# Zero-padded fixed buffers for the probabilities, one add per join, and another point for placing transposed keys, in a sliding-window attention and MLP kernel

## The chip, the cores and the metric

The kernel runs on one core of a Trainium2 chip. The metric is the device time of one execution in microseconds. Six executions of the kernel before gave a median of 327.75 us, from 327.45 to 328.67. A core has five engines, each with a queue of its own that it works through in order: TensorE (PE; its weight loads are listed apart as PEld), VectorE (DVE), ScalarE (ACT), GpSimd (POOL) and SyncE (SP, which here only issues DMAs).

## What is computed

Attention over a window of 32 positions to either side, for 8 batches, 8 heads, 576 tokens and 64 features, and then a two-layer MLP over the 4608 tokens:

```python
scores = scale * np.matmul(q, k.transpose(0, 1, 3, 2))
mask = np.abs(pos[:, None] - pos[None, :]) <= window          # window = 32
scores = np.where(mask, scores, -1000000000.0)
attn = np.exp(scores - np.max(scores, axis=-1, keepdims=True))
attn = attn / (np.sum(attn, axis=-1, keepdims=True) + 1e-09)
x = np.matmul(attn, v)                                        # heads side by side: 4608 x 512
h = x @ w_in                                                  # 512 x 2048
out = np.maximum(0.01 * h, h) @ w_out                         # 2048 x 512
```

## The kernel before

**Chunks.** Attention is cut into 64 chunks. A chunk is one batch, one half of its tokens (288) and one pair of heads: chunk i is batch i // 8, half (i // 4) % 2, pair i % 4. The keys of a pair are held in blocks of 64, two heads in one 128 x 128 weight with zeros off the diagonal (`kbd`, and likewise `vbd` for the values), so that one matmul serves both heads. Nine blocks make a sequence. A block of 64 keys meets up to 128 queries, so neighbouring blocks overlap: in a half, the even blocks together cover all 288 queries, and the odd blocks cover 256 of them. A chunk's scores are these two runs side by side, 544 columns (`NCOL`), made by five matmuls (line 242) in the order of the table `WIN` (line 130): even blocks first and odd ones behind, in both halves.

**A chunk's way.** `score` (line 237): five matmuls into PSUM, then ACT takes the exponential (line 248), then POOL multiplies with a band mask of zeros and ones (line 252), which gives the probabilities `pr`, 128 x 544 in bf16. `join` (line 255), from chunk 12 on: DVE adds the odd run to the even one, so that one matmul gives the sums; 256 of the 288 columns are an add of two parts of `pr` (line 263), and the 32 columns that no odd block covers are a copy (line 265). `weighted` (line 268): PE multiplies the joined sums with a matrix of ones (`s`, line 274; for chunks under 12 it does so for the two runs one after the other, lines 276 and 279), and the probabilities with the values (`x`, line 286). DVE takes the reciprocal of `s` (line 292) and multiplies `x` with it into `xT` (line 294). `s` and `x` have one PSUM buffer each, so PE can't write the next `s` before DVE has taken the reciprocal of the last.

**Keys and queries.** They are loaded by SP, cast to bf16 (line 168: on POOL, at the start also on DVE), and transposed: for batches 0 to 2 by PE (line 201), from batch 3 (`BY_DMA`) by DMA (line 187). ACT then copies the transposed queries and keys into token order (lines 209 and 215), and `place_keys` (line 221) has DVE copy each key tile into the two diagonal parts of `kbd` (line 227, two copies). DVE's copy stands in DVE's queue behind what was queued before it, and what comes behind it waits until ACT's copy is there.

**The MLP.** It works on groups of 288 tokens (half a batch): 16 tiles of the hidden layer per group, each four matmuls (line 305) and a leaky ReLU on ACT (line 309), and output tiles of 128 tokens, each 16 matmuls of 512 columns (line 322), evacuated by ACT (line 327) and stored by SP. Its matmuls take most of PE's time, and the attention of later chunks is laid between them.

**Order.** The program's order is each engine's order. A plan (line 494) lists hidden tiles and quarters of output tiles with the time that PE should need for each; before each, `spend` (line 515) takes the attention steps that have come due. `step` (line 361), for chunk i, queues: the join of chunk i+1; the placing of keys that still wait; transposes that are due; the score of chunk i+2 (in batches from 3 on with its keys' transposes and their placing ahead of it); `weighted(i)`; placing again; then casts, DMA transposes and loads for later batches. Beside the steps, in output tiles at every odd turn, `spend` has ACT copy one more tile of queries or keys that a DMA has transposed (line 532), and right behind it `place_keys` is called (line 533). Engines wait for each other by semaphores that are derived from what each instruction reads and writes.

**Buffers.** `pr` and `both` come from a pool of four buffers each (line 52).

Of the kernel before, what the change touches and what calls it, by code (L numbers as in the profile page):

```python
# [10 lines left out]
BF16 = mybir.dt.bfloat16  # L11
AF = mybir.ActivationFunctionType
# [4 lines left out]
def kernel(  # L17
# [12 lines left out]
    nc = tc.nc  # L30

    B, H, S, D = q.shape
    W = 32
    scale = 1.0 / float(D) ** 0.5
# [5 lines left out]
    HALF = S // 2  # L40
    DMC = DMODEL // 128
    FFC = DFF // 128
    NCOL = 544
# [3 lines left out]
    const = ctx.enter_context(tc.tile_pool(name="const", bufs=1))  # L47
    fload = ctx.enter_context(tc.tile_pool(name="fload", bufs=1))
    cast = ctx.enter_context(tc.tile_pool(name="cast", bufs=1))
    attn = ctx.enter_context(tc.tile_pool(name="attn", bufs=2))  # L50
    kt = ctx.enter_context(tc.tile_pool(name="kt", bufs=4))
    prob = ctx.enter_context(tc.tile_pool(name="prob", bufs=4))
    tdma = ctx.enter_context(tc.tile_pool(name="tdma", bufs=1))
    outp = ctx.enter_context(tc.tile_pool(name="outp", bufs=4))
    PS = bass.MemoryType.PSUM
# [48 lines left out]
    ones_bd = const.tile([128, 128], BF16)  # L104
# [13 lines left out]
    def clear(t, p):  # L118
# [8 lines left out]

    WIN = [  # L130
        [(0, 0, 96), (2, 96, 128), (4, 224, 64), (1, 32, 128), (3, 160, 128)],
        [(4, 288, 64), (6, 352, 128), (8, 480, 96), (5, 288, 128), (7, 416, 128)],
    ]
    ODD = [32, 0]

    win = const.tile([128, 3, 128], BF16)
    nc.gpsimd.memset(win, 1.0)
    for lo in (0, 64):
        w = win[lo:lo + 64]
        nc.gpsimd.affine_select(  # L140
            out=w, in_=w, compare_op=ALU.is_ge, fill=0.0,
# [3 lines left out]
            out=w, in_=w, compare_op=ALU.is_ge, fill=0.0,  # L145
            base=2 * W, channel_multiplier=1, pattern=[[0, 3], [-1, 128]],
        )
    win_f = win.rearrange("p n c -> p (n c)")
    mask = [const.tile([128, NCOL], BF16, name=f"mask{i}") for i in range(2)]

    def make_masks():
        for hf in range(2):
            lo = W * (hf + 1)
            nc.gpsimd.tensor_copy(out=mask[hf][:, 0:HALF], in_=win_f[:, lo:lo + HALF])
            nc.gpsimd.tensor_copy(out=mask[hf][:, HALF:NCOL], in_=win_f[:, 0:NCOL - HALF])


    RING = 4 * HALF
# [7 lines left out]
    def cast_qk(b, p, q_eng=None):  # L166
        for eng, src, dst in ((q_eng or nc.gpsimd, qf, qb), (nc.gpsimd, kf, kb)):
            eng.tensor_copy(  # L168
                out=dst[:, p], in_=src[b, p].rearrange("p a (c d) -> p c a d", d=D),
            )  # L170
# [10 lines left out]
    BY_DMA = 3  # L181
    qkT, asked = {}, {}

    def transpose_dma(b, p):
        for which, src in (("q", qb), ("k", kb)):
            t = tdma.tile([128, RUN, 96], BF16, name=f"{which}T{p}")
            nc.sync.dma_start_transpose(out=t, in_=src[:, p].rearrange("p c a d -> p (c a d)"))
            qkT[b, p, which] = t
        asked[b, p] = state["done"]
# [29 lines left out]
    unplaced = []  # L219

    def place_keys():

        while unplaced:
            b, p, kT = unplaced.pop(0)
            for a in range(2):
                r = slice(64 * a, 64 * a + 64)
                nc.vector.tensor_copy(  # L227
                    out=kbd[b % 2][r, p, :, r],
                    in_=kT[r].rearrange("p (n j) -> p n j", j=64),
                )  # L230

    probs = {}

    def where(i):
        return i // 8, (i // 4) % 2, i % 4

    def score(i):
        b, hf, p = where(i)
        ps = scps.tile([128, 1024], FP32, name="ps")
        c0 = 512 - HALF  # L240
        for blk, q0, n in WIN[hf]:
            nc.tensor.matmul(  # L242
                ps[:, c0:c0 + n], kbd[b % 2][:, p, blk],
                qT[b][:, p, q0:q0 + n], start=True, stop=True,
            )
            c0 += n
        e = attn.tile([128, NCOL], BF16, name="e")
        nc.scalar.activation(  # L248
            out=e, in_=ps[:, 512 - HALF:512 - HALF + NCOL], func=AF.Exp, scale=scale,
        )  # L250
        pr = prob.tile([128, NCOL], BF16, name="pr")
        nc.gpsimd.tensor_mul(pr, e, mask[hf])  # L252
        probs[i] = pr, None

    def join(i):


        hf = where(i)[1]
        pr = probs[i][0]
        both = prob.tile([128, HALF], BF16, name="both")  # L260
        o0 = ODD[hf]
        o1 = o0 + NCOL - HALF
        nc.vector.tensor_add(both[:, o0:o1], pr[:, o0:o1], pr[:, HALF:NCOL])  # L263
        rest = slice(0, o0) if o0 else slice(o1, HALF)
        nc.vector.tensor_copy(out=both[:, rest], in_=pr[:, rest])  # L265
        probs[i] = pr, both

    def weighted(i):
        b, hf, p = where(i)
        pr, both = probs.pop(i)  # L270
        x = xps.tile([128, HALF], FP32, name="x")
        s = xps.tile([128, HALF], FP32, name="s")
        if both is not None:
            nc.tensor.matmul(s, ones_bd, both, start=True, stop=True)  # L274
        else:
            nc.tensor.matmul(
                s, ones_bd, pr[:, 0:HALF], start=True, stop=False, skip_group_check=True,
            )
            nc.tensor.matmul(
                s[:, ODD[hf]:ODD[hf] + NCOL - HALF], ones_bd, pr[:, HALF:NCOL],  # L280
                start=False, stop=True, skip_group_check=True,
            )
        c0 = 0
        for n_, (blk, q0, n) in enumerate(WIN[hf]):
            a = q0 - HALF * hf
            nc.tensor.matmul(  # L286
                x[:, a:a + n], vbd[b % 2][:, p, blk, :], pr[:, c0:c0 + n],
                start=(n_ == 0), stop=(n_ == len(WIN[hf]) - 1), skip_group_check=True,
            )
            c0 += n  # L290
        r = attn.tile([128, HALF], FP32, name="r")
        nc.vector.reciprocal(r, s)  # L292
        t0 = (b * S + hf * HALF) % RING
        nc.vector.tensor_mul(xT[:, p, t0:t0 + HALF], x, r)  # L294
# [58 lines left out]
    def step_transposes(upto):  # L353
        while state["tp"] < min(upto, 8 * B):
            b = state["tp"] // 8
            if b not in t_parts:
                t_parts[b] = transposes(b)
            next(t_parts[b])
            state["tp"] += 1

    def step():


        i = state["done"]
        b, r = i // 8, i % 8
        if JOINED - 1 <= i < NC - 1:
            join(i + 1)
        place_keys()
        if b > 0:
            upto = 8 * (b + 1) + (PLAN[b > 1][0][r] if b + 1 < BY_DMA else 0)  # L370
            step_transposes(max(upto - 1, 8 * (b + 1)))
        if i < 7:
            score(i + 1)
        elif 8 <= i < NC - 2:
            nb, _, np_ = where(i + 2)
            if nb >= BY_DMA:
                step_transposes(8 * nb + 2 * np_ + 2)
                place_keys()
            score(i + 2)
        weighted(i)  # L380
        place_keys()
        if b > 0:
            step_transposes(upto)
        if 0 < b < B - 1:
            for p in PLAN[b > 1][1][r] if b + 1 <= BY_DMA else ():
                cast_qk(b + 1, p)
                if b + 1 == BY_DMA:
                    transpose_dma(b + 1, p)
                if b + 2 < B:
                    load_qk(b + 2, p)  # L390

            n, p = (b + 1, 3) if r == 0 else (b + 2, r - 4)
            if p in range(4 if r == 0 else 3) and BY_DMA < n < B:
                step_transposes(8 * (n - 1) + 2 * p + 2)
                place_keys()
                cast_qk(n, p)
                transpose_dma(n, p)
                if n + 1 < B:
                    load_qk(n + 1, p)
            for p in PLAN[b > 1][2][r]:  # L400
                cast_v(b + 1, p)
                if b + 2 < B:
                    load_v(b + 2, p)
        state["done"] += 1
# [97 lines left out]
    at, t = {}, 0.0  # L502
# [10 lines left out]
    turn = 0  # L513

    def spend(us):
        nonlocal clock, turn
        while due and due[0] <= clock:
            due.pop(0)
            i = state["done"]
            if i < 11:  # L520
                cast_v(1, i - 7)

            if i < 12:
                load_qk(2, i - 8)
            step()
            if 10 <= i < 14:
                load_v(2, i - 10)

        b, p = state["tp"] // 8, state["tp"] % 8 // 2
        turn += 1  # L530
        if kind == "o" and turn % 2 and b >= BY_DMA and (b, p, "k") in qkT and state["done"] > asked[b, p] + 2:
            step_transposes(state["tp"] + 1)
            place_keys()
        clock += us

    for us, kind, g, f in plan:
        if kind == "h":
            spend(us)
            h_tile(g, f)
        elif f == 0:  # L540
            o_tile(g, lambda: spend(O_US))
# [28 lines left out]
```

## Time and profile before

The profiled execution took 327.71 us; its span, from the first instruction to the last, was 326.0 us.

| what | value |
| --- | --- |
| median of 6 runs | 327.75 us |
| profiled execution, and its span | 327.71 us, 326.0 us |
| reciprocals (line 292, DVE) | 64 x 1955 ns |
| mask multiplies (line 252, POOL) | 64 x 1216 ns |
| placing of keys (line 227, DVE) | 64 x 446 ns, and 24.9 us of waiting for ACT's key copies |
| reciprocals waiting for PE's `s` (line 274) | 35.5 us, 34 times |
| hidden layer on PE (line 305) | 1024 matmuls, 133.1 us |
| output layer on PE (line 322) | 592 matmuls, 130.1 us |
| granted TensorE clock | full speed throughout |

How to read the views that follow. The page's first part gives the busy time of each engine and its share of the span. In the part on groups, a line has the source line, the engine, the operation, the output and inputs by the program's names, their form, the count, then busy time in all and the mean of one in ns, and after the second bar the time that the engine was idle just before them. The table by stages has, for each stretch of the span, its length and then for PE, PEld, DVE, ACT and POOL the busy time with the number of instructions, and after these the granted clock, the DMA share and GB/s. The list of waits has the waiting line, what it waited for, the total in us, the number of times and the longest. A timeline has start, length, engine, line, operation and count, and in brackets the idle time before it with what ended it. Matmul ends are modelled, so spacings on PE are better read from start to start.

### The profile page before, as it was taken

The page shows a single profiled execution, that of the slowest core. Times are in us where ns is not written, and L with a number is a line of the kernel's source. Part 1 is how long each engine was busy: PE and PEld are TensorE (multiplying, and loading weights), DVE is VectorE, ACT ScalarE, POOL GpSimd, SP SyncE. Part 2 cuts the span into 40 slices and gives each one's busy share as a digit, 9 for nine tenths or more (in the row PEclk, how much of TensorE's full clock was granted, in tenths as well). Part 3 has the DMA queues.
Part 4 walks back from the last instruction along what each step waited for, and adds up shares of the span by engine and source line. Part 5 has one row for each costly group of instructions (what it writes and reads, how often), then busy time and mean ns, then how long its engine had stood idle before and what let it go on. Part 6 is the DMA issues. An engine that isn't in the chain of part 4 may idle for free.

```text
span 326.0 us, 6609 instructions
## 1 busy us (share of the span) xinstructions
PE 306.7 (94%) x2485; PEld 205.3 (63%) x2485; DVE 224.6 (69%) x310; ACT 224.6 (69%) x432; POOL 179.9 (55%) x213
## 2 busy tenths in 40 slices
PE   1587999999999998999999999999999999999995
PEld 1345785576675755667675767666675857676653
DVE  5389843888767969698758979687849766565100
ACT  5684794375668797778788888888785847464531
POOL 6698839859755876239642686259623544230000
PEclk9999999999999999999999999999999999999999
DMA  8999979999999999917995299917711000010101
GB/s 179 207 196 212 268 191 214 228 256 218 211 201 155 271 205 209 220 66 141 174 240 155 66 194 206 217 68 126 192 38 65 35 32 35 12 55 0 66 32 65
DMA packets 85173, 48.28 MB, mean 148 GB/s; under 512 B 64021, under 2 KB 80661, under 8 KB 85141
## 3 DMA queue, kind: packets, MB, share of 16 engines
q1 hardware_dynamic: 80852, 43.66, 64.7%
q0 software_dynamic: 4288, 4.20, 7.8%
q8 instruction: 19, 0.31, 0.4%
q14 instruction: 14, 0.11, 0.1%
HBM read 36.70 MB, written 9.44 MB: 142 GB/s over the span
## 4 chain that ended last, share of the span: by engine, by line
PE 83%; DVE 7%; DMA 3%; SPq 2%; ACT 2%; issue 1%; POOL 1%; DVEq 0%; POOLq 0%; ACTq 0%
PE mm L322 36%; PE mm L305 35%; DVE r L292 5%; PE x L286 4%; PE ps L242 4%; DMA kf<-in_k_dram 3%; PE s L274 2%; PE tp L201 1%; SPq L83 1%; SPq L72 1%; DVE xT L294 1%; ACT kT L215 1%; DVE both L265 1%; DVE kbd L227 1%; POOL kb L168 1%
## 5 line engine op out<-in xcount | busy, mean ns | idle before, releaser
L292 DVE RECIPROCAL r<-s 128x288 f32<-128x288 f32 x64 | 125.1, 1955 | 41.5 <-PE s L274 35.5
L252 POOL TENSOR_TENSOR pr<-e,mask 128x544 bf16<-128x544 bf16 x64 | 77.8, 1216 | 100.6 <-ACT e L248 80.8
L305 PE MATMUL mm<-xT,w_in_bf 128*128 128x288 bf16 x1024 | 133.1, 286 | 0.0
L322 PE MATMUL mm<-w_out_bf,gT 128*128 128x512 bf16 (+2 forms) x592 | 130.1, 373 | 0.0
L309 ACT ACTIVATE gT<-mm 128x288 bf16<-128x288 f32 x256 | 104.1, 412 | 25.4 <-PE mm L305 9.6
L305 PEld LDWEIGHTS <-w_in_bf 128*128 128x128 bf16 x1024 | 98.3, 98 | 23.9
L322 PEld LDWEIGHTS <-gT 128*128 128x128 bf16 x592 | 56.4, 98 | 59.8
L327 ACT ACTIVATE o_sb<-mm 128x512 f32<-128x512 f32 (+2 forms) x37 | 21.7, 585 | 55.6 <-PE mm L322 55.6
L248 ACT ACTIVATE e<-ps 128x544 bf16<-128x544 f32 x64 | 39.8, 622 | 11.1 <-PE ps L242 10.5
L227 DVE COPY kbd<-kT 64x576 bf16<-64x576 bf16 x64 | 28.5, 446 | 25.5 <-ACT kT L215 24.9
L178 POOL CAST vbd<-vf 64x576 bf16<-64x576 f32 x58 | 38.5, 664 | 2.1 <-DMA vf<-in_v_dram 0.3
L294 DVE TENSOR_TENSOR xT<-x,r 128x288 bf16<-128x288 f32 x64 | 29.3, 458 | 6.7
L168 POOL CAST kb<-kf 96x768 bf16<-96x768 f32 x32 | 27.6, 863 | 10.3 <-DMA kf<-in_k_dram 10.3
L286 PE MATMUL x<-pr,vbd 128*128 128x128 bf16 (+2 forms) x320 | 26.3, 214 | 1.3 <-DVE xT L294 1.2
L242 PE MATMUL ps<-qT,kbd 128*128 128x128 bf16 (+2 forms) x320 | 26.8, 216 | 0.0
L242 PEld LDWEIGHTS <-kbd 128*128 128x128 bf16 x320 | 20.9, 101 | 8.2
L286 PEld LDWEIGHTS <-vbd 128*128 128x128 bf16 x320 | 20.9, 99 | 6.6 <-DVE xT L294 2.5
L209 ACT ACTIVATE qT<-qT 128x576 bf16<-128x576 bf16 x20 | 23.6, 1181 | 0.0
L215 ACT ACTIVATE kT<-kT 128x576 bf16<-128x576 bf16 x20 | 23.6, 1180 | 0.0
L265 DVE COPY both<-pr 128x32 bf16<-128x32 bf16 x52 | 22.7, 436 | 0.0
L263 DVE TENSOR_TENSOR both<-pr 128x256 bf16<-128x256 bf16 x52 | 21.0, 405 | 0.6
L168 POOL CAST qb<-qf 96x768 bf16<-96x768 f32 x24 | 19.7, 819 | 0.0
(39 smaller groups left out, 110.9 us busy)
## 6 DMA issues: line engine op xcount, KB each, us to landing
qf<-in_q_dram SPq DMA_DIRECT2D x32, 288.0 KB, 4.5
kf<-in_k_dram SPq DMA_DIRECT2D x32, 288.0 KB, 5.5
vf<-in_v_dram SPq DMA_DIRECT2D x64, 144.0 KB, 5.1
out_dram<-o_sb SPq DMA_DIRECT2D x35, 256.0 KB, 2.2
w_in_bf<-in_moe_w_in_dram POOLq DMA_DIRECT2D x8, 256.0 KB, 6.5
w_out_bf<-in_moe_w_out_dram POOLq DMA_DIRECT2D x4, 512.0 KB, 12.7
qT<-qb SPq DMA_TRANSPOSE x20, 4.3
kT<-kb SPq DMA_TRANSPOSE x20, 3.9
```

The lines of the kernel that those rows point to most:

```text
L168: eng.tensor_copy(out=dst[:, p], in_=src[b, p].rearrange("p a (c d) -> p c a d", d=D),)
L178: nc.gpsimd.tensor_copy(out=vbd[b % 2][r, p, :, r], in_=vf[b, p][r])
L227: nc.vector.tensor_copy(out=kbd[b % 2][r, p, :, r], in_=kT[r].rearrange("p (n j) -> p n j", j=64),)
L242: nc.tensor.matmul(ps[:, c0:c0 + n], kbd[b % 2][:, p, blk], qT[b][:, p, q0:q0 + n], start=True, stop=True,)
L248: nc.scalar.activation(out=e, in_=ps[:, 512 - HALF:512 - HALF + NCOL], func=AF.Exp, scale=scale,)
L252: nc.gpsimd.tensor_mul(pr, e, mask[hf])
L286: nc.tensor.matmul(x[:, a:a + n], vbd[b % 2][:, p, blk, :], pr[:, c0:c0 + n], start=(n_ == 0), stop=(n_ == len(WIN[hf]) - 1), skip_group_c ...
L292: nc.vector.reciprocal(r, s)
L294: nc.vector.tensor_mul(xT[:, p, t0:t0 + HALF], x, r)
L305: nc.tensor.matmul(h[:, 0:HALF], w_in_bf[:, c, ts(f, 128)], xT[:, c, ds(t0, HALF)], start=(c == 0), stop=(c == DMC - 1),)
L309: nc.scalar.activation(out=gT[:, f, ds(t0, HALF)], in_=h[:, 0:HALF], func=AF.Prelu, alpha=0.01,)
L322: nc.tensor.matmul(o[:, lo:hi], gT[:, f, ds(128 * j % RING, 128)], w_out_bf[:, f, lo:hi], start=(f == 0), stop=(f == FFC - 1),)
```

## The change

The probabilities move from the pool into one fixed tile of six buffers, each with 32 columns ahead of the 544 and 32 behind, which are set to zero once. `i % 6` picks the buffer. For the first half, the odd blocks now come first (256 columns) and the even ones behind; for the second half the order stays. With that, the 288 columns that begin in the pad (first half) or end in it (second half) are the odd run with zeros where no odd block reaches, and `join` is one add of 288 columns with 288. `both` gets a pool of its own with two buffers. The masks, the exponential's source and the sums of chunks under 12 follow the new order.

Keys: `step` no longer places at its head from batch 2 on, and places ahead of a score only when a key tile of that very pair waits; and in `spend` a tile whose copy was queued at an odd turn is placed at the next even turn, a quarter of an output tile later in the program.

```diff
+    joined = ctx.enter_context(tc.tile_pool(name="joined", bufs=2))
-    prob = ctx.enter_context(tc.tile_pool(name="prob", bufs=4))
...
+    PAD = 32
+    SPLIT = [HALF - PAD, HALF]
     WIN = [
-        [(0, 0, 96), (2, 96, 128), (4, 224, 64), (1, 32, 128), (3, 160, 128)],
+        [(1, 32, 128), (3, 160, 128), (0, 0, 96), (2, 96, 128), (4, 224, 64)],
         [(4, 288, 64), (6, 352, 128), (8, 480, 96), (5, 288, 128), (7, 416, 128)],
     ]
-    ODD = [32, 0]
...
+    NPROB = 6
+    prob = const.tile([128, NPROB, NCOL + 2 * PAD], BF16)
+    nc.vector.memset(prob[:, :, 0:PAD], 0.0)
+    nc.vector.memset(prob[:, :, PAD + NCOL:], 0.0)
...
     def score(i):
...
-        c0 = 512 - HALF
+        lo = c0 = 512 - SPLIT[hf]
...
         nc.scalar.activation(
-            out=e, in_=ps[:, 512 - HALF:512 - HALF + NCOL], func=AF.Exp, scale=scale,
+            out=e, in_=ps[:, lo:lo + NCOL], func=AF.Exp, scale=scale,
         )
-        pr = prob.tile([128, NCOL], BF16, name="pr")
+        pr = prob[:, i % NPROB, PAD:PAD + NCOL]
         nc.gpsimd.tensor_mul(pr, e, mask[hf])
...
         hf = where(i)[1]
-        pr = probs[i][0]
-        both = prob.tile([128, HALF], BF16, name="both")
-        o0 = ODD[hf]
-        o1 = o0 + NCOL - HALF
-        nc.vector.tensor_add(both[:, o0:o1], pr[:, o0:o1], pr[:, HALF:NCOL])
-        rest = slice(0, o0) if o0 else slice(o1, HALF)
-        nc.vector.tensor_copy(out=both[:, rest], in_=pr[:, rest])
-        probs[i] = pr, both
+        lo = PAD * hf
+        t = prob[:, i % NPROB]
+        both = joined.tile([128, HALF], BF16, name="both")
+        nc.vector.tensor_add(both, t[:, lo:lo + HALF], t[:, lo + HALF:lo + 2 * HALF])
+        probs[i] = probs[i][0], both
...
     def step():
...
-        place_keys()
+        if b < BY_DMA - 1:
+            place_keys()
...
             if nb >= BY_DMA:
                 step_transposes(8 * nb + 2 * np_ + 2)
-                place_keys()
+                if any(key[:2] == (nb, np_) for key in unplaced):
+                    place_keys()
             score(i + 2)
...
     def spend(us):
...
         if kind == "o" and turn % 2 and b >= BY_DMA and (b, p, "k") in qkT and state["done"] > asked[b, p] + 2:
             step_transposes(state["tp"] + 1)
+        elif kind == "o" and turn % 2 == 0:
             place_keys()
```

## The prediction

> **What bounds the kernel now.** I read the engine totals first, then TensorE (PE) by stages, then the list of what PE waited for, and last the instructions of the one stage where it waits.
>
> ```profile
> span 326.0 us, 6609 instructions
> PE 306.7 (94%) x2485; PEld 205.3 (63%) x2485; DVE 224.6 (69%) x310; ACT 224.6 (69%) x432; POOL 179.9 (55%) x213
> ```
>
> PE is at 94%; VectorE (DVE), which the change relieves, is at 69%. So time taken off DVE is worth nothing by itself. It counts only where PE stood still because DVE was late. The stage table gives busy time per stretch (start:end, length, then each engine):
>
> ```profile
> 40.00:124.00 84.00, 83.85 (x717) 55.88 (x716) 59.47 (x84) 59.31 (x119) 60.46 (x71) 1.00 1.04 216
> 124.00:131.00 7.00, 5.29 (x52) 3.75 (x49) 6.75 (x11) 4.44 (x11) 3.74 (x5) 1.00 1.18 198
> 131.00:305.00 174.00, 174.00 (x1380) 116.33 (x1378) 129.64 (x182) 126.58 (x242) 84.02 (x93) 1.00 0.54 110
> ```
>
> PE (first pair) is full from 40 to 124 us and again from 131 to the end of attention. Between them it loses 7.00 - 5.29 = 1.71 us while DVE is busy 6.75 of 7.00. That hole is the only place where a quicker join can pay. The waits of PE from 36 us to the end say the same: nothing but DVE, and little of it.
>
> ```profile
> PE s L274 <- DVE r L292: 1.0, 1, 1.0
> PE x L286 <- DVE xT L294: 0.9, 4, 0.3
> ```
>
> **The hole, instruction by instruction.** The timelines of DVE, POOL and PE over it (start us, length us). Step i handles chunk i: DVE joins chunk i+1, then PE scores i+2 and runs s and x of i, then DVE inverts (r) and multiplies (xT) i.
>
> ```profile
> 120.90 0.91 DVE L227 COPY kbd<-kT 64x576 bf16<-64x576 bf16 x2 [1.55 <-ACT kT L215]
> 121.84 0.29 DVE L263 TENSOR_TENSOR both<-pr 128x256 bf16<-128x256 bf16 x1
> 121.99 1.22 POOL L252 TENSOR_TENSOR pr<-e,mask 128x544 bf16<-128x544 bf16 x1 [1.47 <-issue]
> 122.05 1.19 DVE L265 COPY both<-pr 128x32 bf16<-128x32 bf16 x1
> 123.15 1.94 DVE L292 RECIPROCAL r<-s 128x288 f32<-128x288 f32 x1
> 125.15 0.28 PE L274 MATMUL s<-both,ones_bd 128*128 128x288 bf16 x1 [1.00 <-DVE r L292]
> 125.57 0.90 DVE L227 COPY kbd<-kT 64x576 bf16<-64x576 bf16 x2
> 125.71 0.41 PE L286 MATMUL x<-pr,vbd 128*128 128x96 bf16 x5 [0.28 <-DVE xT L294]
> 126.50 0.81 DVE L263 TENSOR_TENSOR both<-pr 128x256 bf16<-128x256 bf16 x1
> 127.23 0.79 DVE L265 COPY both<-pr 128x32 bf16<-128x32 bf16 x1
> 127.94 1.94 DVE L292 RECIPROCAL r<-s 128x288 f32<-128x288 f32 x1
> 130.50 0.41 PE L286 MATMUL x<-pr,vbd 128*128 128x96 bf16 x5 [0.28 <-DVE xT L294]
> ```
>
> This is chunks 23 to 25. DVE waits for ACT's key copy until 120.88, places keys, joins chunk 24 and only at 123.15 begins the reciprocal whose s was issued at 119.93. The 32-column copy took 1.19 us, against a median of 169 ns (view of the tile `both`): POOL's mask multiply, of 1.22 us, had begun at 121.99, between add and copy. Counted by starts, PE reached s24 at 123.98 (score at 123.74 plus 0.24) and issued it at 125.15: 1.17 lost. x24 lost 125.71 - 125.27 = 0.44; s25 129.94 - 129.63 = 0.31; x25 130.50 - 130.06 = 0.44. Together 2.36 us, a little more than the 1.71 that busy time shows.
>
> **Part 1, one add for add and copy.**
>
> ```profile
> L265 DVE COPY both<-pr 128x32 bf16<-128x32 bf16 x52 | 22.7, 436 | 0.0
> L263 DVE TENSOR_TENSOR both<-pr 128x256 bf16<-128x256 bf16 x52 | 21.0, 405 | 0.6
> ```
>
> Removed: 52 copies, 22.7 us of DVE. The add grows from 256 to 288 columns. Unhindered, add start to reciprocal start is 0.28 us now (106.98 to 107.26), of which the add takes 0.21. The 288-column add is not in the trace: from below it costs no more than the present add; from above, the 128x288 multiply of line 294 (one operand f32 in PSUM) takes 458 ns, +0.18. I take +0.02 (0.21 x 32/256), since the nearest row is the same operation, type and memory. So DVE sheds about 52 x 0.42 = 22 us, nearly all beside a full PE, where it is worth 0. In the hole:
>
> - Join 24 starts at 121.84 as now (its keys come from ACT, unchanged), and the reciprocal at 121.84 + 0.23 = 122.07 instead of 123.15. s24 follows a reciprocal's start by 2.00 (123.15 to 125.15): 124.07, while PE is there at 123.98: loss 0.09. x24 follows it by 2.56 (123.15 to 125.71): 124.63.
> - Place of the next keys 2.42 after the reciprocal: 124.49. Join 25, 0.93 later: 125.42. POOL's next mask multiply runs from 125.19 to the next POOL instruction at 126.35, so this add must wait. Now the add of 126.50 waits likewise for the POOL instruction that hands over at 127.11, and DVE's next starts at 127.23, 0.12 later. So the reciprocal starts at 126.35 + 0.12 + 0.02 = 126.49 instead of 127.94.
> - s25 at 128.49; PE, coming from x24 over 28 matmuls, a score and s (0.24 + 3.43 + 0.24), is there at 128.54: no loss. x25 at 126.49 + 2.56 = 129.05 instead of 130.50.
>
> Sum: 1.45 us earlier. It persists: behind it DVE waits 1.80 us for PE before the reciprocal of 135.23, and PE is full to the end.
>
> At this place a rule speaks against counting on the join. The row: the add's longest is 809 ns, its shortest 279. The Trainium skill, page "SBUF — State Buffer", section "Who interferes with whom", says that a DVE instruction with two SBUF inputs contends with a GpSimd instruction that reads SBUF, and the one that comes second is blocked for the other's whole length. The trace agrees (809 is no intrinsic length); by the rule the change halves the occasions but not the price of one, and if each of the two joins met a whole 1.22 us multiply the sum would be a gain of about 0.6 instead of 1.45.
>
> **Part 2, keys placed later.** Writing out, from the two programs, what each engine is given in which order: PE, ACT, POOL and SP get the same order. On DVE, of 52 joins and the placements, four pairs change places. Placements 2,1 and 2,2 (batch, pair) go ahead of joins 16 and 17; their keys leave ACT at 77.88 and 83.30, before DVE is free (79.10 and 84.16), and the reciprocals after them wait for PE anyway (0.66 at 81.72, 1.78 at 87.53): 0. Placements 5,1 and 7,2 go behind a join and a reciprocal, at 172 and 244 us; there DVE stood 2.74 us waiting for ACT, beside a full PE: 0 on the path. Their keys are first read five or six steps later (chunks 41 and 58). If that cover were gone, each would cost at most its own 0.9 us. Elsewhere, a placement queued a quarter of an output tile later, with no DVE instruction between, runs at the same instant. In the hole DVE's order is unchanged. No DMA is issued earlier or later.
>
> **Part 3, buffers.** Two memsets of 192 columns at the start, before the first query cast (4.60). Not in the trace; 64 columns cost 112 ns and 2304 cost 1978, so 0.11 to 0.25 each. The first key transposes wait for POOL until 6.01 and the next for DMA (0.70 at 9.21): 0; uncovered, 0.5. Six buffers instead of four, and two for the joined sums: join i+1 needs s of i-1 done, and DVE has already waited for it in its reciprocal: 0.
>
> **Part 4, order of blocks in the first half.** The same widths, now ending with the 64-wide one instead of 128. Below: nothing to gain. Above: weight loads follow each other by 0.063 us (five in 0.35 at 106.83, the last of 0.098), a 64-wide matmul by about 0.029 (0.2156 us per 512 and 0.1225 per 288 columns give 0.42 ns a column and 2.5 ns): 0.034 x 64 = 2.2 us. I take 0: the group takes 0.24 in both halves (110.62 to 110.86, 115.14 to 115.38), with the 64-wide matmul first in one and third in the other.
>
> **Forecast.** The profiled execution took 327.71 us (span 326.0, 1.7 around it), close to the median of 327.75; less 1.45 gives 326.3, 0.44% faster. About 0.2% (0.66 us) is what a measurement can tell from no change.
>
> **Rivals.**
> - *POOL first at join 24.* The multiply of 121.99 starts 0.15 us after the add; were it first, the reciprocal would start at 123.15 + 0.14, s24 at 125.29, and the second join would wait for the handover at 127.11: reciprocal 127.25, x25 at 129.89. Gain 0.6: 327.1. Against it: both start times hang on the same ACT copy ending at 120.88. Chance 0.12.
> - *Join 25 meets no POOL* (the multiply comes after 125.42): x25 at PE's own pace, 128.65, gain 1.85: 325.9. It needs a shift of only 0.23. Chance 0.13.
> - *Weight loads behind the 64-wide matmul show.* In the 32 first-half chunks, score and x lose up to 0.034 each: 327.71 - 1.45 + 2.2 = 328.5, slower; it decides from 1.45/64 = 0.023 a time, and passes 0.2% at 0.033. Half of it gives about 327.4. Chances 0.09 and 0.06.
> - *The change isn't what it says: one fixed tile is tracked as a whole.* Then x of chunk i would wait for the mask multiply of i+2: exp 0.62 and multiply 1.21 after each score, some 1.9 us x 54 steps, about 430 us. Against it: kbd, xT and gT are single tiles too, and PE reads one part while others write the rest without a wait. Chance 0.05.
> - The forecast has the rest: 0.55.
>
> Faster 0.55 + 0.13 = 0.68; same 0.12 + 0.06 = 0.18; slower 0.14. The range takes in the forecast with its bounds (an add of 458 ns leaves 1.45 - 0.36 = 1.1), both joins' cases, and half the loads: 325.5 to 327.4.
>
> **What would show it.** Right: line 265 gone, its add near 0.30 unhindered, DVE down by some 20 us, PE's idle between 124 and 131 us down from 1.71 to about 0.6 (x24 and x25 still wait for DVE), the end of everything behind it 1.4 to 1.5 earlier, DVE's wait for ACT's keys smaller only at two places. Wrong: a score or x group of a first half taking more than 0.24; the add at chunk 24 lasting over 1 us; a new wait of PE elsewhere.

## The result, and the profile after

The changed kernel takes 325.1 us (median of 21 executions, 324.06 to 326.0) against 327.42 for the kernel before (47 executions): ratio 0.9928, 95% interval 0.9917 to 0.9940, which is 2.4 us less (2.0 to 2.7). The forecast was 326.3 with a range of 325.5 to 327.4; the direction and the place of the gain were right, its size was not.

The totals of the changed kernel's page, and its table by stages (stretch, length, then busy time of PE, PEld, DVE, ACT and POOL with instruction counts, granted clock, DMA share, GB/s):

```profile
span 323.7 us, 6565 instructions
PE 306.2 (95%) x2485; PEld 205.4 (63%) x2485; DVE 208.9 (65%) x260; ACT 224.6 (69%) x432; POOL 180.2 (56%) x213
```

```profile
40.00:124.00 84.00, 83.51 (x713) 55.44 (x711) 55.69 (x72) 59.47 (x119) 60.98 (x71) 1.00 1.01 217
124.00:131.00 7.00, 6.75 (x63) 5.41 (x64) 6.75 (x9) 5.21 (x13) 4.04 (x4) 1.00 1.22 243
131.00:303.00 172.00, 172.00 (x1364) 114.69 (x1363) 117.57 (x144) 125.28 (x239) 83.20 (x92) 1.00 0.50 109
```

PE's busy time is what it was; the hole, 5.29 busy of 7.00 before, is nearly closed: its head now lies just ahead of 124 us, and from 123 to 130 PE is busy for 6.50 of 7.00. PE's waits from 36 us on, where `s` stood with 1.0 us and `x` with 0.9:

```profile
PE x L295 <- DVE xT L303: 0.7, 3, 0.3
```

The join, as a group (busy us, mean ns) and by the view of its tile (shortest, median, longest ns):

```profile
L273 DVE TENSOR_TENSOR both<-prob 128x288 bf16<-128x288 bf16 x52 | 22.8, 439 | 0.6
```

```profile
L273 DVE TENSOR_TENSOR both<-prob x52: 296/309/1146, 63.2 to 292.4; 128x288 bf16<-128x288 bf16 x52
```

43.7 us of add and copy became 22.8; a 288-column add takes 17 ns more than one of 256 had (296 against 279). DVE's total fell by only 15.7, mainly since each copy began before its add had ended (by 0.08 us in the prediction's rows) and the sums of groups count that twice. And the hole (start, length; chunks 23 to 25, as the prediction showed them):

```profile
120.29 0.91 DVE L238 COPY kbd<-kT 64x576 bf16<-64x576 bf16 x2 [1.54 <-ACT kT L226]
121.23 0.31 DVE L273 TENSOR_TENSOR both<-prob 128x288 bf16<-128x288 bf16 x1
121.40 1.22 POOL L263 TENSOR_TENSOR prob<-e,mask 128x544 bf16<-128x544 bf16 x1 [1.45 <-issue]
121.46 1.95 DVE L301 RECIPROCAL r<-s 128x288 f32<-128x288 f32 x1
123.14 0.40 PE L253 MATMUL ps<-qT,kbd 128*128 128x128 bf16 x5
123.46 0.28 PE L282 MATMUL s<-both,ones_bd 128*128 128x288 bf16 x1
124.03 0.41 PE L295 MATMUL x<-prob,vbd 128*128 128x128 bf16 x5 [0.28 <-DVE xT L303]
124.82 1.15 DVE L273 TENSOR_TENSOR both<-prob 128x288 bf16<-128x288 bf16 x1
125.89 1.94 DVE L301 RECIPROCAL r<-s 128x288 f32<-128x288 f32 x1
128.45 0.41 PE L295 MATMUL x<-prob,vbd 128*128 128x128 bf16 x5 [0.22 <-DVE xT L303]
```

Join 24 starts 0.17 us ahead of POOL's multiply and is through; join 25 meets the next multiply and lasts 1.15. Measured from the hole's score (123.74 before, 123.14 after) to x of chunk 25, the hole took 6.76 us and takes 5.31: 1.45 less, the forecast sum. So two profiles that differ by 2.3 us hold 1.45 in the hole; 0.60 had come before its head, and the last 0.24 comes behind PE's last matmul. The experiments ask what the rest is.

### The profile page after: what moved, and what is told of

Its sections match the earlier page's. It is cut to its first block, busy times and chain, and to the rows that moved or that the text cites. A ratio compares the mean times of both kernels' runs of the same rounds, so it can differ in the third digit from the quotient of the medians.

```text
span 323.7 us, 6565 instructions
## 1 busy us (share of the span) xinstructions
PE 306.2 (95%) x2485; PEld 205.4 (63%) x2485; DVE 208.9 (65%) x260; ACT 224.6 (69%) x432; POOL 180.2 (56%) x213
## 4 chain that ended last, share of the span: by engine, by line
PE 79%; DMA 7%; DVE 6%; SPq 2%; ACT 2%; POOL 1%; issue 1%; DVEq 0%; POOLq 0%; ACTq 0%
PE mm L331 36%; PE mm L314 32%; DMA kf<-in_k_dram 7%; DVE r L301 4%; PE x L295 4%; PE ps L253 4%; PE s L282 2%; SPq L72 1%; SPq L83 1%; PE tp L212 1%; DVE xT L303 1%; POOL kb L179 1%; ACT kT L226 1%; DVE kbd L238 1%; DVE both L273 0%
## 5 line engine op out<-in xcount | busy, mean ns | idle before, releaser
L263 POOL TENSOR_TENSOR prob<-e,mask 128x544 bf16<-128x544 bf16 x64 | 77.7, 1214 | 98.7 <-ACT e L259 80.3
L238 DVE COPY kbd<-kT 64x576 bf16<-64x576 bf16 x64 | 28.5, 446 | 20.6 <-ACT kT L226 17.9
L295 PE MATMUL x<-prob,vbd 128*128 128x128 bf16 (+2 forms) x320 | 26.3, 214 | 1.4 <-DVE xT L303 1.3
L253 PEld LDWEIGHTS <-kbd 128*128 128x128 bf16 x320 | 21.8, 101 | 8.0
L295 PEld LDWEIGHTS <-vbd 128*128 128x128 bf16 x320 | 21.8, 99 | 5.1 <-issue 1.9
L273 DVE TENSOR_TENSOR both<-prob 128x288 bf16<-128x288 bf16 x52 | 22.8, 439 | 0.6
L282 PE MATMUL s<-both,ones_bd 128*128 128x288 bf16 x52 | 14.9, 286 | 0.0
```

Source lines behind the costliest of these rows:

```text
L238: nc.vector.tensor_copy(out=kbd[b % 2][r, p, :, r], in_=kT[r].rearrange("p (n j) -> p n j", j=64),)
L253: nc.tensor.matmul(ps[:, c0:c0 + n], kbd[b % 2][:, p, blk], qT[b][:, p, q0:q0 + n], start=True, stop=True,)
L295: nc.tensor.matmul(x[:, a:a + n], vbd[b % 2][:, p, blk, :], pr[:, c0:c0 + n], start=(n_ == 0), stop=(n_ == len(WIN[hf]) - 1), skip_group_c ...
```

## The experiments

Theories: **hole only** (1.45 us is the change, the rest is scatter of the start); **start** (the new buffers, memsets or block order also shorten the first 36 us); **placement** (the later keys carry the rest); and, after the first runs, **amplified** (a microsecond in the hole is worth more in the time). "Stretch" is the hole from its score to x of chunk 25. e12, the kernel before with an unused tile of the new buffers' size and the two memsets, has no result: there is no room for that tile beside the old buffers.

| kernel | stretch, us | median, us | ratio to before, 95% interval |
| --- | --- | --- | --- |
| before again (e1) | 6.76 | 327.36 | 1.0003 (0.9984 to 1.0022) |
| join only (e2) | 5.31 | 324.80 | 0.9939 (0.9917 to 0.9961) |
| placement only (e3) | 6.76 | 327.06 | 0.9999 (0.9978 to 1.0020) |
| all, but add and copy (e4) | 6.76 | 327.02 | 1.0000 (0.9984 to 1.0016) |
| all, but add and copy at 24, 25 (e5) | 6.76 | 327.26 | 0.9991 (0.9970 to 1.0011) |
| one add at 24, 25 only (e6) | 5.32 | 325.28 | 0.9940 (0.9916 to 0.9964) |
| all, a key behind the reciprocal (e7) | 4.40 | 324.02 | 0.9910 (0.9879 to 0.9941) |
| all, again (e8) | 5.31 | 325.30 | 0.9945 (0.9921 to 0.9968) |
| three more reciprocals (e9) | 12.68 | 332.68 | 1.0165 (1.0136 to 1.0194) |
| old join, a key behind (e10) | 5.17 | 325.70 | 0.9949 (0.9929 to 0.9969) |
| e7 again (e11) | 4.39 | 324.70 | 0.9918 (0.9894 to 0.9943) |
| all, tile in another pool (e13) | 5.31 | 325.78 | 0.9949 (0.9928 to 0.9970) |
| block order only (e14) | 6.76 | 327.17 | 0.9993 (0.9977 to 1.0008) |
| all, third time (e15) | 5.31 | 325.35 | 0.9927 (0.9903 to 0.9951) |

**Parts of the change.** e1 is the kernel before.

> The kernel before, unchanged, for a second profile and for how far two sets of runs of one program lie apart. The measured gain of the change (2.3 us) is 0.9 more than the 1.45 us seen in the hole of chunks 23 to 25; in the two profiles 0.6 of it lies before 36 us, where the changed kernel's first loads landed earlier. If that 0.6 is chance (theory: hole only), this second profile shows the first hidden-layer matmul anywhere between 28.0 and 28.8 us, and the ratio is 1.000 within 0.0015. If it is the change (theory: start), it comes at 28.7 again.

e2 puts the three `place_keys()` calls back where they were; e3 moves only them:

```diff
-        place_keys()
+        if b < BY_DMA - 1:
+            place_keys()
...
             step_transposes(state["tp"] + 1)
+        elif kind == "o" and turn % 2 == 0:
             place_keys()
```

> New buffers, new block order and the one add; keys placed where they were before. Theory hole only and theory start: all of the gain, 2.3 us against before (within 0.5), no difference from the whole change. Rival, that the later placement carries the 0.9 that the hole doesn't explain: 1.45 us against before.

> Only the later placement, with the old buffers and the join in two instructions. Theories hole and start: 0 against before, within 0.4 us, and the hole at 124 to 131 us as before (1.7 us of PE idle). Rival, placement carries part: 0.9 us faster.

e4 keeps buffers, pads and order, and makes the join of two instructions again (`o0` to `o1` are the 256 columns that both runs cover, `rest` the other 32, `even` the run of the even blocks):

```diff
-        nc.vector.tensor_add(both, t[:, lo:lo + HALF], t[:, lo + HALF:lo + 2 * HALF])
...
+        nc.vector.tensor_add(both[:, o0:o1], t[:, lo + o0:lo + o1], t[:, lo + HALF + o0:lo + HALF + o1])
...
+        nc.vector.tensor_copy(out=both[:, rest], in_=even[:, rest])
```

> The whole change, but each join is an add of 256 columns and a copy of 32 again, in the new buffers and order. Theory hole only: 0 against before, within 0.4 us. Theory start (block order, buffers or memsets make the first 36 us shorter whatever the join): 0.6 to 0.9 us faster, with the first hidden-layer matmul at about 28.1 us.

The placement alone gives nothing that can be measured, the join alone the whole gain: the placement theory falls. With two instructions in the new buffers the median is that of the kernel before, which speaks against the start theory; but e4's first hidden-layer matmul came at 27.46 us, as early as that theory asked. The second profile of before has it at 28.68, like the first (28.73), which both theories allow.

**Which joins?** e5 has add and copy at chunks 24 and 25 and one add everywhere else, e6 the reverse (an `if` on chunks 24 and 25 around the two forms).

> The whole change, but chunks 24 and 25, and only they, are joined by an add of 256 and a copy of 32 columns. Theory hole: the gain of 1.45 us falls away in the profile (6.76 us from the score at the hole's head to x of chunk 25, instead of 5.31), and against before the kernel is 0 faster if the hole is all there is, and 0.9 faster if the other 50 joins give the part of the gain that the profiles don't show.

> The reverse: one add at chunks 24 and 25 only, add and copy at the other 50. Theory hole: 5.31 us from the hole's score to x of 25, and 1.45 us faster than before, or the whole 2.3 if the hole is all there is; the rival that the other joins carry 0.9 us of the gain leaves 1.45.

> The changed kernel again, on the chip of these runs, for their comparison and for a second profile of its start: 2.3 us faster than before if the measured gain is stable, 1.45 if the first measurement had 0.9 from chance. The hole's 5.31 us are the same in either case.

Two joins of 52 carry the gain; the other 50 give nothing that these runs can tell. In e5 the copy at chunk 24 again meets POOL, and the reciprocal waits:

```profile
121.62 0.29 DVE L276 TENSOR_TENSOR both<-prob 128x256 bf16<-128x256 bf16 x1
121.83 1.20 DVE L279 COPY both<-prob 128x32 bf16<-128x32 bf16 x1
122.94 1.94 DVE L309 RECIPROCAL r<-s 128x288 f32<-128x288 f32 x1
```

**The cause of the hole.** e7 is the changed kernel with the keys of batch 3, pair 3 placed in step 23 behind `weighted`; e11 repeats it. e10 does the same to the kernel before, with its old join.

```diff
-        elif kind == "o" and turn % 2 == 0:
+        elif kind == "o" and turn % 2 == 0 and state["done"] != 23:
             place_keys()
```

> The whole change, and the keys of batch 3, pair 3 placed behind the reciprocal of chunk 23 instead of ahead of it and of join 24, so that this reciprocal needn't wait for ACT's key copy. The profile of the changed kernel leaves 0.91 us lost at s24, x24 and x25. If the late reciprocal behind the key copy causes it, PE has no idle left between 119 and 133 us and the kernel is 0.9 us faster than the changed one (324.2). If another engine holds the stage, the loss moves and the time stays.

> The kernel before, with its joins of add and copy, and only the keys of batch 3, pair 3 placed behind the reciprocal of chunk 23. If the hole is made by that reciprocal standing behind the key copy, and not by the join's length as such, this alone brings back between 1.4 us (the 32-column copy of join 25 loses POOL's port by 0.03 us) and 2.4 us (it wins it): faster than before by that much, without any change to the join. If the join itself is the cause, 0.

> The changed kernel with that key placement behind the reciprocal, a second time, as it was the fastest. Theory chance: 1.45 + 0.91 = 2.36 us faster than before, ratio 0.9928. Rival, amplified: 3.4 us, ratio 0.9896.

The stage of e7, and the reciprocal of chunk 23 there, which now waits for PE and not PE for it:

```profile
120.00:127.00 7.00, 7.00 (x60) 4.83 (x59) 6.12 (x10) 6.53 (x13) 5.23 (x6) 1.00 1.10 231
```

```profile
119.02 1.96 DVE L301 RECIPROCAL r<-s 128x288 f32<-128x288 f32 x1 [0.27 <-PE s L282]
```

The stretch falls to 4.40, 0.91 less, and PE has no idle in it. In the time, e7 and e11 are 0.7 us below the changed kernel (means of 12 and of 40 executions, 324.5 and 325.2). e10 shows that the old join alone doesn't make the hole: with it, moving one pair of key copies shortens the stretch by 1.59 (5.17) and the time by about as much. The hole needs both. Over e7's 4.40, where PE never waits, the late reciprocal alone costs 0.91 (the changed kernel), the old join alone 0.77 (e10), and both together 2.36 (before). What e10 still loses comes from its 32-column copy, which begins 0.03 us after POOL's multiply, the lower of the two cases expected:

```profile
124.70 1.21 POOL L252 TENSOR_TENSOR pr<-e,mask 128x544 bf16<-128x544 bf16 x1 [0.63 <-POOL vbd L178]
```

```profile
124.73 1.21 DVE L265 COPY both<-pr 128x32 bf16<-128x32 bf16 x1
127.85 0.28 PE L274 MATMUL s<-both,ones_bd 128*128 128x288 bf16 x1 [0.17 <-DVE r L292]
```

**A known dose.** e9 puts three reciprocals into join 24, written to a tile that nothing reads (`last[0]` is the `r` of the chunk before).

```diff
...
+        if i == 24:
+            for _ in range(3):
+                nc.vector.reciprocal(scratch, last[0])
```

> The whole change, with three more reciprocals on VectorE between join 24 and the reciprocal of chunk 23 (into a tile that nothing reads): a known dose of lateness in the hole. From the trace of the changed kernel: 3 x 2.05 us later there, of which POOL's wait at join 25 absorbs 0.85, so the stretch from the hole's score to x of chunk 25 grows by 5.3 us, from 5.31 to 10.6. Theory chance (a microsecond in the hole is a microsecond in the time; the rest of the measured gain is scatter of the start): about 5.3 us slower than the changed kernel, which is 3.3 slower than before. Rival, amplified (the hole's 1.45 us gave 2.1 in the time, so each is worth 1.45): 7.7 slower than the changed kernel.

It is 7.6 us slower than the changed kernel (means of 6 and of 40 executions, 332.8 and 325.2), near the number that "amplified" had named. But the profile shows the same 7.37 in the stretch itself (12.68 against 5.31): 5.80 of lateness at x24, and 1.95 because x24 and the 28 hidden-layer matmuls behind it ran slowly (the 28 took 5.18 us instead of 3.43); x25's own wait of 0.38 is gone. The timeline of PE and the stage behind the wait, with the granted clock third from the end:

```profile
129.13 0.40 PE L287 MATMUL s<-both,ones_bd 128*128 128x288 bf16 x1 [5.72 <-DVE r L306]
...
130.14 5.34 PE L320 MATMUL mm<-xT,w_in_bf 128*128 128x288 bf16 x28
```

```profile
129.00:132.00 3.00, 2.71 (x14) 1.61 (x14) 2.85 (x6) 0.41 (x1) 0.00 (x0) 0.50 1.27 229
```

So what the profile's stretch gains or loses, the time gains or loses, here too; neither theory had the clock in its number, and "amplified" falls in spite of its figure.

**What is left.** All executions of the six kernels with the 5.31 us stretch (the change three times, e2, e6, e13: 66) have a mean of 325.31 us, all those of the kernel before (153) 327.42. The difference of 2.1 (standard error 0.12) is 0.65 more than the hole. e14 has only the new block order, with the old pool and two instructions; e13 takes the fixed tile from `const` into the otherwise empty pool behind the load buffers, and e15 is the changed kernel beside it.

> The changed kernel with the fixed tile in another pool, behind the load buffers instead of ahead of them. Theory start by address: the 0.3 to 0.6 us are lost, 1.5 to 1.8 us faster than before. Theories memsets, order or chance: as the changed kernel in this set of runs, within 0.4.

> The new block order and the later placement, with the old pool of probabilities, no pads, no memsets, and add and copy in the join. Theory start by block order: 0.3 to 0.6 us faster than before. Theories address, memsets, chance: 0 within 0.3. The hole takes 6.76 us in every case.

> The changed kernel on the chip of these runs, to compare e13 with. If the part beyond the hole is real, 2.1 us faster than before (ratio 0.9936); if it was chance in the sets so far, 1.45 (0.9956).

The block order alone gives 0.2 us, which its interval doesn't tell from 0. e13 is 0.4 us behind e15, with intervals that overlap: inconclusive. e4 and e5, with the new layout and the old stretch, have a mean of 327.1 over 24 executions, 0.3 under before. So part of the 0.65 may be the layout; at a standard error of 0.12, the scatter of single executions is too little for all of it.

The profiles show where it sits. From x of chunk 25 to the last matmul all sixteen take 191.7 us, and from there to the end 3.5 to 3.9, so most of it lies ahead of the hole. There the first hidden-layer matmul starts between 26.79 us (e2) and 29.21 (e3), in each of them 11.6 to 11.9 us after POOL begins to cast the fourth key tile, and this cast waits for the tile's load. Before, and in the changed kernel:

```profile
16.89 0.82 POOL L168 CAST kb<-kf 96x768 bf16<-96x768 f32 x1 [0.83 <-DMA kf<-in_k_dram]
```

```profile
16.45 0.82 POOL L179 CAST kb<-kf 96x768 bf16<-96x768 f32 x1 [0.67 <-DMA kf<-in_k_dram]
```

The cast begins at 15.9 to 17.4 us in the five profiles with the old buffers and at 15.1 to 16.5 in the eleven with the new. The ranges overlap, and no run separates addresses, memsets and chance: why that load lands earlier **stays open**. From the first hidden-layer matmul to the hole's score it takes 94.8 to 95.9. One reason for this spread is the granted clock, in the stage from 25 to 30 us of e8 and of the changed kernel's first profile:

```profile
25.00:30.00 5.00, 4.17 (x28) 2.55 (x25) 4.46 (x4) 1.26 (x3) 4.30 (x5) 0.67 1.24 206
```

```profile
25.00:30.00 5.00, 3.87 (x40) 2.76 (x39) 4.79 (x5) 1.67 (x4) 4.94 (x6) 1.00 1.20 180
```

## Why the prediction was right and wrong

**What bounds the kernel: right from 40 us on.** There PE is full outside the hole; 50 quicker joins beside a full PE gave nothing that can be measured (e5), two in the hole everything (e6). Ahead of 36 us PE is not full, and there the prediction looked at the memsets alone.

**Part 1, the join in the hole: right to 0.01 us.** Behind the hole's score, s24, x24, s25 and x25 were forecast at 0.33, 0.89, 4.80 and 5.31 us; the profile has 0.32, 0.89, 4.81 and 5.31. It wasn't luck: the five other profiles with one add at both chunks have 5.31 or 5.32. What was unknown, the longer add, was taken at +0.02 and is +0.017. Of the two adds, the one that began 0.23 us after POOL's multiply lasted 1.15 us, and the one that began 0.17 us ahead of it 0.31. The Trainium skill's page "SBUF — State Buffer" ("Who interferes with whom") says that a DVE instruction with two SBUF inputs contends with a GpSimd instruction that reads SBUF, and that the order of issue decides who is blocked; the rows agree. DVE's total fell by 15.7 us and not by the 22 of the prediction, which took no account of the overlap of copy and add.

**Part 2, placement: right, 0.** Its own run (e3) is at 0.9999. DVE's wait for ACT's keys fell from 24.9 to 17.9 us in the changed kernel and to 21.0 in e3, without an effect on e3's time.

**Part 3, memsets: priced right** (138 ns each, within 0.11 to 0.25); that they and the new addresses are worth 0 on the start is neither shown nor refuted. **Part 4, block order: right** as far as can be told (e14, 0.2 us); score and x of a first half still take 0.24 and 0.25 from start to start, so the rival of the weight loads falls. So do the whole-tile rival and both rivals about POOL at joins 24 and 25.

**The step that failed is the last, from the sum to the time.** "Less 1.45 gives 326.3" took the hole's gain off one profiled execution of 327.71 us and put 0 on everything else, and the range held only the unknowns of the sum. The mechanism and the 1.45 were right; the time came out 1.2 below the forecast. Of this, 0.3 is the base: over 47 executions the median before is 327.42. The other 0.9 (0.65 over all runs) is in no term of the sum. The runs show most of it ahead of the hole, where the work starts when a load lands and at the clock that is granted; its cause stays open. The prediction named 0.66 us as what a measurement can tell, and the six executions shown already spread over 1.2 us, but neither went into the range. By that spread, as an estimate, the range had to be some 0.5 us wider on either side.

The prediction also said that x24 and x25 would still wait for DVE, which they do (0.28 and 0.22), and PE's idle in the hole is 0.50 where it said about 0.6. It had read that the reciprocal stood in DVE's queue behind a key copy that waited for ACT, but took this as given and did not ask what moving the copy would be worth: in the stretch 1.6 us without the change (e10), and 0.9 with it (e7).

## What to carry to other kernels

A quicker instruction on a side engine is worth only what the bounding engine lost to it: find the few places where it waited, and replay those by start times. Here that gave the gain of the stage in advance to a hundredth of a microsecond, though not that of the whole kernel. Then ask what stands in front of the late instruction in its queue: where an in-order engine waits for another's copy, reordering can help, and here it gave as much as shortening the work did. Set a profile's sum against the spread of the runs, too, and not only against their median.

## What was not expected

After an idle time of 5.72 us (e9) PE's granted clock was 0.50 in the next 3 us, and 28 matmuls cost 1.75 us more. It had fallen within the wait, which began at 123.4 us: 1.00 from 123 to 126, 0.95 from 126 to 127 and 0.50 from 127 to 128, so some 3.5 us into it. The Trainium skill, page "TensorE: Matmul & The Clock Gate", section "Part 1: The HAM clock gate", says that the clock is halved after an idle window of about 3.4 us; the run agrees. The wait of 1.0 us in the hole of the kernel before left it at 1.00. In some executions the clock also dips to 0.67 between 25 and 30 us, with no difference in the program.

The fastest version measured is the changed kernel with the keys of batch 3, pair 3 placed behind the reciprocal (e7, e11): ratio 0.9910 (0.9879 to 0.9941) and 0.9918 (0.9894 to 0.9943) to the kernel before.
